# FNet mixing and a channel MLP on one core: z split untransposed, and transposed by the DMA that loads it

## The chip, the core and the metric

The kernel runs on one core of a Trainium2 chip. The metric is the device time of one execution in microseconds: the median of three runs is 1991.27 us (1990.38 to 1991.77).

## The reference

`A_x` has 2048 tokens of 1024 features; the MLP's hidden width is 3584. All is f32.

```python
mod = (silu(c) @ w_mod).reshape(1, 6, 1, 1024)
sa, ca, ga, sb, cb, gb = (mod[:, i] for i in range(6))
h = layernorm(x) * (1 + ca) + sa
a, b = h @ dft_hid_re.T, h @ dft_hid_im.T
x = x + ga * (dft_seq_re @ a - dft_seq_im @ b)
h = layernorm(x) * (1 + cb) + sb
h = layernorm(h)                                  # the MLP's own
x = x + gb * (gelu(h @ w1 + b1) @ w2 + b2)
```

## The kernel before

Every large product runs in fp16 with split operands: a f32 number is a high part (rounded to fp16) and a low part (the rest), and three matmuls (high x high, high x low, low x high) stand for one. On top of it lies one level of the Strassen-Winograd scheme: of four quadrants of each operand, sums and differences are formed on VectorE (DVE) in f32, and seven smaller products replace eight. The seven are always taken in the order 0, 1, 2, 4, 3, 6, 5.

The program has four large stages on TensorE (PE):

- gemm1 (L1112, L1162): the sequence DFT, whose result u goes to DRAM.
- gemm2 (L1394): the DFT over features, in eight blocks b of 256 tokens. A block has 14 pieces (seven products, real and imaginary) of 12 matmuls. After each block, `ln_tasks` does both layernorms of its 256 tokens on DVE and ScalarE (ACT), in the buffer `wb(b)`: two buffers of 8 KB per partition, used in turn. x is loaded into the same buffer first (`load_xw`, L1368), and added by DVE at L1253. The result, w in the code and z in the names, has tokens on the 128 partitions and 1024 features in a row, for two tiles of 128 tokens (n = 0 and 1).
- gemm3 (L1585): 28 steps g, 14 for each half of the tokens. A step multiplies 256 columns of w1 with 1024 tokens of z: seven products of 12 matmuls. w1 is the stationary operand and z the moving one, so z must have features on the partitions.
- gemm4 (L1694): after two steps of gemm3 one step of gemm4 with w2.

So z is transposed once. `turn_tile` (L1296) does it on TensorE: eight f32 transposes of 128 by 128 for a tile, with the identity `ident`, into two banks of PSUM (6 and 7 in gemm2). ACT copies the tile back (L1306, or L1864 for the last three tiles) to `zt(b, n)`. `z_tasks` then forms the quadrant sums (L411) in `zt`, and the high (L386, ACT) and low parts (L396, DVE) of the seven combinations; POOL stores each (L1328) to `zc_d[h][m]` in DRAM, h the half of the tokens and m the product. `load_zc` (L1336) loads one product's 1 MB: 128 partitions with 8 KB in a row. The first seven loads are issued while block 7 of gemm2 runs, since they go to the room of its right operands `dp`; the other seven (`reload`) while step 13 of gemm3 runs, each when that step has used the product's old contents.

The order on each engine is made when the program is built. `Task` has an engine, an estimated cost and what it depends on; streams of tasks have a due time; `pick` takes, by a model of the engines' clocks, what may start next. Loads are issued by SP in such an order, with 8 of its DMAs in flight at most (each waits for the one eight before it); stores of z by POOL. Both queues are in order. In gemm2 the function `turns` asks after every piece whether a tile of z is ready by the model, and puts its transposes there. `load_xw(b)` waits until the transposes of block b - 2 have read the buffer.

## Time and profile before

| | |
|---|---|
| median of three runs | 1991.27 us |
| profiled execution, first to last instruction | 1990.4 us |
| TensorE busy, weight loads busy | 1969.1, 896.5 us |
| DVE, ACT, POOL busy | 1417.3, 851.1, 190.5 us |
| f32 transposes | 128 (L1296) |
| gemm1, gemm2, first gemm3, first gemm4 begin | 47.4, 658.3, 961.9, 1021.2 us |
| granted TensorE clock | 0.999 |

The profiled execution has no other time than that span; the median of the runs lies 0.9 us above it. Times in the profile count from the first instruction. A line number is the one in the kernel before; in the changed kernel the same statements have numbers that are lower by 3 (up to L1279) or by 17 to 53 (after it).

### The profile page before, as it was taken

How to read it: one execution, taken by the hardware profiler on the slowest of the kernel's cores; microseconds unless marked ns; L12 is line 12 of the kernel's file. 1: busy time of each engine (PE TensorE's matmuls, PEld its weight loads, DVE VectorE, ACT ScalarE, POOL GpSimd, SP SyncE). 2: the span in 40 equal slices, each digit the busy share in tenths (PEclk: the TensorE clock that was granted, in tenths of full speed). 3: DMA queues.
4: the chain of work that ended last, by engine and by line, in shares of the span. 5: the costliest groups of instructions: out<-in, count | busy, mean ns of one | idle time of the engine just before them, and what ended most of it. 6: DMA issues, size and time to landing. Idle time of an engine off the chain costs nothing. (4 is left out here: it accounts for less than half of the span.)

```text
span 1990.4 us, 23735 instructions
## 1 busy us (share of the span) xinstructions
PE 1969.1 (99%) x9082; PEld 896.5 (45%) x9082; DVE 1417.3 (71%) x1795; ACT 851.1 (43%) x1091; POOL 190.5 (10%) x282
## 2 busy tenths in 40 slices
PE   9999999999999999999999999999999999999999
PEld 3444444444444444444444444444444444444443
DVE  2977886997984467777588999999873353553566
ACT  2853432344542245554477566466233322312311
POOL 0002212221220112221020000000000000000000
PEclk9999999999999999999999999999999999999999
DMA  9138677678779777877765454453477332432323
GB/s 380 53 97 281 236 264 275 246 298 329 249 256 364 271 261 256 282 244 277 276 218 190 171 199 168 145 175 146 169 231 216 117 97 83 127 101 69 111 74 85
DMA packets 139363, 402.42 MB, mean 202 GB/s; under 512 B 15536, under 2 KB 15536, under 8 KB 134640
## 3 DMA queue, kind: packets, MB, share of 16 engines
q1 hardware_dynamic: 112528, 309.92, 45.3%
q0 software_dynamic: 26720, 90.98, 12.8%
q8 instruction: 71, 1.16, 0.2%
q14 instruction: 44, 0.36, 0.1%
HBM read 262.95 MB, written 137.89 MB: 201 GB/s over the span
## 5 line engine op out<-in xcount | busy, mean ns | idle before, releaser
L1694 PE MATMUL ps<-arena 128*128 128x512 f16 x2352 | 511.1, 379 | 2.8 <-DVE arena L1740 1.5
L1585 PE MATMUL ps<-arena 128*128 128x512 f16 x2352 | 510.2, 379 | 2.2 <-ACT arena L1607 2.2
L1162 PE MATMUL ps<-arena 128*128 128x512 f16 x2016 | 435.5, 379 | 1.4 <-DMA arena<-s 1.4
L1694 PEld LDWEIGHTS <-arena 128*128 128x128 f16 x2352 | 229.9, 98 | 281.5 <-issue 3.8
L1585 PEld LDWEIGHTS <-arena 128*128 128x128 f16 x2352 | 230.1, 98 | 279.4 <-issue 2.5
L1740 DVE SCALAR_TENSOR_TENSOR arena<-ps,i4c,arena 128x1024 f32<-128x1024 f32 x179 | 229.3, 1281 | 144.4 <-PE ps L1694 143.1
L1162 PEld LDWEIGHTS <-arena 128*128 128x128 f16 x2016 | 197.1, 98 | 239.5 <-DMA arena<-s 1.9
L1394 PE MATMUL ps<-arena 128*128 128x512 f16 x1344 | 292.4, 379 | 1.9 <-DMA arena<-u 1.9
L386 ACT ACTIVATE arena<-arena,shc 128x512 f16<-128x512 f32 (+1 forms) x115 | 115.9, 1018 | 277.3 <-PE ps L1694 184.6
L1394 PEld LDWEIGHTS <-arena 128*128 128x128 f16 x1344 | 131.4, 98 | 158.0 <-DMA arena<-u 2.4
L1112 PE MATMUL ps<-arena 128*128 128x512 f16 x768 | 167.4, 379 | 7.2 <-ACT arena L635 2.0
L411 DVE TENSOR_TENSOR arena<-arena 128x512 f32<-128x512 f32 (+1 forms) x228 | 171.0, 753 | 4.1
L681 ACT ACTIVATE arena<-arena 128x1024 f16<-128x1024 f32 x100 | 104.1, 1050 | 150.8 <-PE ps L1162 111.4
L398 DVE SCALAR_TENSOR_TENSOR arena<-arena,shc 128x512 f16<-128x512 f32 (+1 forms) x115 | 128.7, 1122 | 38.4 <-ACT arena L386 38.3
L684 DVE SCALAR_TENSOR_TENSOR arena<-arena 128x1024 f16<-128x1024 f32 x100 | 128.6, 1303 | 18.5 <-ACT arena L681 18.5
L1611 DVE TENSOR_TENSOR arena<-arena,ps 128x512 f32<-128x512 f32 x84 | 57.5, 685 | 110.7 <-PE ps L1585 106.5
L1604 ACT ACTIVATE arena<-arena,b1s,i1c 128x512 f32<-128x512 f32 x84 | 68.3, 813 | 137.0 <-DVE arena L1611 137.0
L1112 PEld LDWEIGHTS <-arena 128*128 128x128 f16 x768 | 74.7, 98 | 99.9 <-ACT arena L635 4.0
L773 ACT ACTIVATE arena<-arena 128x1024 f16<-128x1024 f32 x56 | 57.7, 1047 | 60.9 <-DVE arena L1186 18.8
L776 DVE TENSOR_TENSOR arena<-arena 128x1024 f16<-128x1024 f32 x56 | 66.9, 1218 | 14.6 <-ACT arena L773 14.6
L386 ACT ACTIVATE arena<-arena,s1c 128x512 f16<-128x512 f32 (+1 forms) x70 | 60.8, 884 | 36.9 <-DVE arena L411 25.9
L398 DVE SCALAR_TENSOR_TENSOR arena<-arena,s1c 128x512 f16<-128x512 f32 (+1 forms) x70 | 66.3, 959 | 11.0 <-ACT arena L386 10.8
(159 smaller groups left out, 1418.8 us busy)
## 6 DMA issues: line engine op xcount, KB each, us to landing
w<-arena SPq DMA_DIRECT2D x64, 512.0 KB, 5.0
arena<-w SPq DMA_DIRECT2D x119, 256.0 KB, 2.7
u<-arena POOLq DMA_DIRECT2D x56, 512.0 KB, 5.5
arena<-u SPq DMA_DIRECT2D x112, 256.0 KB, 4.0
arena<-w SPq DMA_DIRECT2D x56, 512.0 KB, 3.4
arena<-s SPq DMA_DIRECT2D x48, 512.0 KB, 7.6
arena<-in_cre_dram SPq DMA_DIRECT2D x32, 512.0 KB, 7.3
arena<-in_cim_dram SPq DMA_DIRECT2D x32, 512.0 KB, 5.2
```

The lines of the kernel that those rows point to most:

```text
L386: act.activation(o[m][0], q(j), AF.Copy, **sc)
L398: dve.scalar_tensor_tensor(o[m][1], q(j), scale, o[m][0], op0=ALU.mult, op1=ALU.subtract)
L411: dve.tensor_tensor(q(d), q(a), q(b), op=op)
L681: h = Task("act", 1.15, lambda: act.activation(o[:, :, 0], s2, AF.Copy, scale=SC), list(deps) + free)
L684: dve.scalar_tensor_tensor(o[:, :, 1], s2, SC, o[:, :, 0], op0=ALU.mult, op1=ALU.subtract)
L1112: pe.matmul(bank_of(d_), hleft(d_, s, kp, a), cop(n)[:, s, b], start=(kp == 0 and s == 0 and a == 0 and b == 0), stop=(kp == 7 and s == 1 ...
L1162: pe.matmul(bank_of(st + ch), left, cop(n)[:, s, b], start=(start and kp == 0 and s == 0 and a == 0 and b == 0), stop=(kp == 3 and s == 1 ...
L1394: pe.matmul(bank_of(bk), up(N)[:, c_, a], dp(n)[:, c_, w], start=(start and ri == 0 and c_ == 0 and i == 0), stop=(ri == 1 and c_ == 3 and ...
L1585: pe.matmul(ps.rearrange("p (k t) -> p k t", k=4), w1c[:, m, s, a, d * P : (d + 1) * P], zc(m)[:, b, :, d, :], start=(start and d == 0 and ...
L1604: act.activation(dst, src, AF.Gelu_apprx_tanh, scale=inv, bias=b1s[:, 2 * p + j : 2 * p + j + 1])
L1694: pe.matmul(t[:, j], hidc[:, c_, m, a, k * P : (k + 1) * P], w2c[:, m, c_, w], start=(start and c_ == 0 and n == 0), stop=(c_ == 1 and n = ...
L1740: lambda: dve.scalar_tensor_tensor(dst, ps[b], inv, dst, op0=ALU.mult, op1=ALU.add), kp[b],
```

## The change

The transposes, their copies, the identity and `turns` are gone. `z_tasks` works in place on w itself, with tokens on the partitions, and the stores write that layout. For the last block the layernorm's final ACT operation writes to the place `O_K` directly, where `zt` stood before. `load_zc` issues a transposing DMA: of the 4096 columns of a product, each run of 128 becomes 128 partitions with 128 tokens. The buffer of w is then free for x only when z is split, so `load_xw(b)` waits for the seven combinations of block b - 2. `z_tasks(b)` is handed to the planner after `ln_tasks(b)`, due 40 us later, and has six places for its results.

```diff
@@ ln_tasks
-            f = lambda n=n: act.activation(w[:, n], w[:, n], AF.Identity, scale=r[:, n : n + 1], bias=nm[:, n : n + 1])
+            f = lambda n=n: act.activation(zw(b)[:, n], w[:, n], AF.Identity, scale=r[:, n : n + 1], bias=nm[:, n : n + 1])
...
-    def zt(b, n):
-        return at((O_K if b == NB - 1 else 144) + 4 * n, 1024)
-
-    def turn_tile(b, n, ps):
-
-        for d in range(ND):
-            pe.transpose(ps[:, d * P : (d + 1) * P], wb(b)[:, n, d * P : (d + 1) * P], ident[:, :])
-
-    def turn(b, n):
...
+    def zw(b):
+
+        return at(O_K, 2048).rearrange("p (r e) -> p r e", r=2) if b == NB - 1 else wb(b)
 
     def z_tasks(b):
 
-        e, o = zt(b, 0), zt(b, 1)
+        e, o = zw(b)[:, 0], zw(b)[:, 1]
...
-        places = [O_K + 8 + 2 * k for k in range(4)] if b == NB - 1 else [152, 154, 46 if b == NB - 2 else 182, 216, 218]
+        places = [O_K + 8 + 2 * k for k in range(4)] if b == NB - 1 else [144, 146, 148, 150, 152, 154]
...
-            dst = zc_d[h][m][:, :, k].rearrange("p a c t -> p a (c t)")
+            dst = zc_d[h][m][:, :, k].rearrange("p a c e -> p a (c e)")
...
-            q, outs, None, 512, lambda j: ("zt", b, j % 2), lambda m: ("z", b, m), post=post,
+            q, outs, None, 512, lambda j: ("w", b, j % 2), lambda m: ("z", b, m), post=post,
...
     def load_zc(h, m):
-        sp.dma_start(at(O_ZC[m], 4096, F16), zc_d[h][m].rearrange("p a k c t -> p (a k c t)"))
+        o = at(O_ZC[m], 4096, F16).rearrange("p (n t) -> p n t", t=P)
+        sp.dma_start_transpose(o, zc_d[h][m].rearrange("p a k c e -> p (a k c e)"))
...
-        was = [("turn", b - 2, n) for n in range(2)] if b > 1 else [("g1", opn(3, 5, 3))]
+        was = [("z", b - 2, m) for m in range(7)] if b > 1 else [("g1", opn(3, 5, 3))]
...
     for b in range(NB):
         gemm2(b, each(b))
         push("ln", "ln", ln_tasks(b), clk["pe"] + 10.0)
+        if b < NB - 2:
+            push("z", f"z{b}", z_tasks(b), clk["pe"] + 40.0)
...
-    def turn_late(b, n):
...
-                turn_late(NB - 2, 0)
                 push("z", f"z{NB - 2}", z_tasks(NB - 2), due[3, 1] + 5)
...
-                turn_late(NB - 1, 1)
-                turn_late(NB - 1, 0)
                 push("z", f"z{NB - 1}", z_tasks(NB - 1), due[4, 0] + 10)
```

How it moves the instructions is shown at three places. First SP's queue at the end of gemm2, the loads of the first half. In these names `zc_0` to `zc_6` are z's products, `w_1` is w1's step 1, `u_6_1` and the like are the last left operands of gemm2, and `in_x` is x for a layernorm (here that of block 7). Before:

```order
249 L1346 DMA arena_65<-u_6_1_140 128x1024
250 L1336 DMA arena_65<-zc_0_67 128x4096
251 L1571 DMA arena_65<-w_1_161 128x1024
252 L1368 DMA arena_65<-in_x_dram 128x2x1024
253 L1336 DMA arena_65<-zc_1_68 128x4096
254 L1571 DMA arena_65<-w_1_161 128x1024
255 L1346 DMA arena_65<-u_5_0_137 128x1024
256 L1336 DMA arena_65<-zc_2_69 128x4096
257 L1571 DMA arena_65<-w_1_161 128x1024
258 L1346 DMA arena_65<-u_5_1_138 128x1024
259 L1336 DMA arena_65<-zc_4_71 128x4096
```

And SP's queue at the same place in the changed kernel:

```order
251 L1319 DMA_TRANSPOSE arena_65<-zc_0_67 128x32x128
252 L1527 DMA arena_65<-w_1_161 128x1024
253 L1329 DMA arena_65<-u_6_1_140 128x1024
254 L1319 DMA_TRANSPOSE arena_65<-zc_1_68 128x32x128
...
256 L1329 DMA arena_65<-u_5_0_137 128x1024
257 L1319 DMA_TRANSPOSE arena_65<-zc_2_69 128x32x128
...
259 L1329 DMA arena_65<-u_5_1_138 128x1024
260 L1319 DMA_TRANSPOSE arena_65<-zc_4_71 128x32x128
...
264 L1319 DMA_TRANSPOSE arena_65<-zc_6_73 128x32x128
265 L1527 DMA arena_65<-w_1_161 128x1024
266 L1351 DMA arena_65<-in_x_dram 128x2x1024
267 L1319 DMA_TRANSPOSE arena_65<-zc_5_72 128x32x128
```

The seven loads of z are transposes now, with the same w1 loads between them; the load of x for block 7 has moved from behind the first of them to behind the sixth, and u_6_1 from ahead of the first to behind it.

Second, DVE around the last layernorm, where block 5's splits end before it (L396 low part, L411 quadrant sum, L1416 the adds of gemm2, L1267 and L1253 the first operations of block 7's layernorm, L1611 the first add of gemm3). Before:

```order
714 L1416 TENSOR_TENSOR arena_65<-arena_65,ps 128x512
715 L396 TENSOR_TENSOR arena_65<-arena_65 128x512
716 L411 TENSOR_TENSOR arena_65<-arena_65 128x512
717 L1416 TENSOR_TENSOR arena_65<-arena_65,ps 128x512
718 L411 TENSOR_TENSOR arena_65<-arena_65 128x512
719 L396 TENSOR_TENSOR arena_65<-arena_65 128x512 x3
...
727 L1253 SCALAR_TENSOR_TENSOR arena_65,lns_35_218<-arena_65 128x1024
728 L1267 TENSOR_TENSOR arena_65<-arena_65 128x1024
729 L1253 SCALAR_TENSOR_TENSOR arena_65,lns_35_218<-arena_65 128x1024
730 L1611 TENSOR_TENSOR arena_65<-arena_65,ps 128x512
```

In the changed kernel, DVE at the same place (L393 is the low part, L1399 the adds of gemm2, L1250 the add of x, L1569 the adds of gemm3):

```order
690 L393 TENSOR_TENSOR arena_65<-arena_65 128x512 x3
...
693 L1399 TENSOR_TENSOR arena_65<-arena_65,ps 128x512
...
701 L1399 TENSOR_TENSOR arena_65<-arena_65,ps 128x512
...
716 L1569 TENSOR_TENSOR arena_65<-arena_65,ps 128x512
717 L1264 TENSOR_TENSOR arena_65<-arena_65 128x1024
718 L1250 SCALAR_TENSOR_TENSOR arena_65,lns_34_213<-arena_65 128x1024
719 L1264 TENSOR_TENSOR arena_65<-arena_65 128x1024
720 L1250 SCALAR_TENSOR_TENSOR arena_65,lns_34_213<-arena_65 128x1024
721 L1212 TENSOR_SCALAR lns_34_213<-lns_34_213 128x2
722 L1569 TENSOR_TENSOR arena_65<-arena_65,ps 128x512 x2
```

The last low parts of block 5 now stand ahead of the last two adds of gemm2, and the adds of x behind the first add of gemm3 instead of ahead of it.

Third, TensorE at the end of the third gemm3 step, with the two tiles of block 7 turned before the first gemm4:

```order
8894 L1585 MATMUL ps<-arena_65 128x512
8895 L1296 MATMUL ps<-ident_181,arena_65 128x128 x16
8896 L1694 LDWEIGHTS arena_65
8897 L1694 MATMUL ps<-arena_65 128x512
```

In the changed kernel, TensorE at the same place (L1543 is gemm3, L1652 gemm4):

```order
8880 L1543 MATMUL ps<-arena_65 128x512
8881 L1652 LDWEIGHTS arena_65
8882 L1652 MATMUL ps<-arena_65 128x512
```

The 16 transposes are gone and the matmuls on both sides follow each other; the other 14 places are alike.

40 lines of the change are left out of this document (removed).

## The prediction

> **What bounds the kernel now.** I read the share of busy time first, then who made TensorE wait, then TensorE's own timeline where the change cuts into it.
>
> ```profile
> PE 1969.1 (99%) x9082; PEld 896.5 (45%) x9082; DVE 1417.3 (71%) x1795; ACT 851.1 (43%) x1091; POOL 190.5 (10%) x282
> PE ps L1585 <- ACT arena L1607: 2.2, 1, 2.2
> PE ps L1394 <- DMA arena<-u: 1.9, 1, 1.9
> PE ps L1694 <- DVE arena L1740: 1.5, 2, 1.2
> L1296 PE MATMUL ps<-ident,arena 128*128 128x128 f32 x128 | 16.4, 273 | 0.0
> L1306 ACT ACTIVATE arena<-ps 128x1024 f32<-128x1024 f32 x13 | 13.3, 1023 | 22.7 <-PE ps L1296 22.7
> ```
>
> TensorE is busy for 99% of the span, and its two longest waits (engine, line, who released it, total us) are of about 2 us each. So a microsecond taken out of TensorE's stream is a microsecond of the span, unless something else then arrives late. The 128 transposes (L1296) are in that stream. Their copies out of PSUM (L1306, and three at L1864) are on ACT, which is busy for 43%: these are not on the path.
>
> **What the transposes cost.** The mean of 273 ns is no price, because records of neighbouring matmuls overlap. The price is the distance between starts (start, length, engine, line, count):
>
> ```profile
> 771.45 1.04 PE L1296 MATMUL ps<-ident,arena 128*128 128x128 f32 x8
> 772.32 5.34 PE L1394 MATMUL ps<-arena 128*128 128x512 f16 x24
> 777.50 1.04 PE L1296 MATMUL ps<-ident,arena 128*128 128x128 f32 x8
> ...
> 932.99 23.47 PE L1394 MATMUL ps<-arena 128*128 128x512 f16 x108
> 958.38 2.76 PE L1394 MATMUL ps<-arena 128*128 128x512 f16 x12 [1.92 <-DMA arena<-u]
> 960.98 1.04 PE L1296 MATMUL ps<-ident,arena 128*128 128x128 f32 x8
> 961.86 18.29 PE L1585 MATMUL ps<-arena 128*128 128x512 f16 x84
> ...
> 1019.49 1.91 PE L1296 MATMUL ps<-ident,arena 128*128 128x128 f32 x16
> 1021.23 5.13 PE L1694 MATMUL ps<-arena 128*128 128x512 f16 x23
> ```
>
> Eight transposes take 772.32 - 771.45 = 0.87 us, sixteen take 1021.23 - 1019.49 = 1.74 us. The 24 matmuls behind the first eight take 777.50 - 772.32 = 5.18 us, or 0.216 us each, so 12 of them (one piece of gemm2, one product of gemm3) take 2.59 us. All 16 tiles: 16 x 0.87 = **13.95 us** leave TensorE.
>
> **What is added: 14 transposing loads.** No row of this trace has one, so its price T per load (1 MB, 1.05 MB in decimal) is the unknown. How late a load may be comes from where the plain ones land now:
>
> ```profile
> 935.77 0.32 SPq L1336 DMA_DIRECT2D arena<-zc  x1
> ...
> 957.77 0.32 SPq L1336 DMA_DIRECT2D arena<-zc  x1
> ```
> ```profile
> L1336 SPq DMA_DIRECT2D arena<-zc x1: 319/319/319, 957.8 to 957.8; - x1
> DMA to landing us min/median/max: 14.3/14.3/14.3
> ```
> ```profile
> 945.00:960.00 15.00, 13.08 (x62) 5.79 (x60) 9.19 (x23) 4.43 (x7) 3.75 (x6) 1.00 1.03 415
> ```
> ```profile
> L1336 SPq DMA_DIRECT2D arena<-zc x1: 320/320/320, 1425.7 to 1425.7; - x1
> DMA to landing us min/median/max: 4.8/4.8/4.8
> ```
> ```profile
> 1425.74 8.09 SPq L1336 DMA_DIRECT2D arena<-zc  x4
> ```
> ```profile
> w<-arena SPq DMA_DIRECT2D x64, 512.0 KB, 5.0
> arena<-w SPq DMA_DIRECT2D x119, 256.0 KB, 2.7
> ...
> arena<-u SPq DMA_DIRECT2D x112, 256.0 KB, 4.0
> ...
> out_dram<-arena POOLq DMA_DIRECT2D x28, 512.0 KB, 5.5
> ...
> arena<-zc SPq DMA_DIRECT2D x14, 1024.0 KB, 6.9
> ...
> arena<-in_x_dram SPq DMA_DIRECT2D x8, 1024.0 KB, 7.4
> ```
> ```profile
> 1422.96 36.42 PE L1585 MATMUL ps<-arena 128*128 128x512 f16 x168
> ```
>
> The first seven loads are issued between 935.77 and 957.77, during the last block of gemm2. The last one lands at 957.77 + 14.3 = 972.1, and its product (the seventh of the first gemm3) starts at 961.86 + 6 x 2.59 = 977.4. The DMA engines are full there (share 1.03, 415 GB/s), so a plain 1 MB costs 1.05 / 0.415 = 2.5 us of queue and 256 KB costs 0.63. A plain load into an idle queue (the first of the second half, at 1425.7) lands after 4.8 us, so about 4.8 - 2.5 = 2.3 us are latency. In the second half each load is issued when gemm3 number 13 has done that product, and is needed 84 x 0.216 = 18.1 us later, in number 14.
>
> Bounds for T: below, a plain load, 2.5 us. Above, 6.9 us, the median from issue to landing of all 14 plain loads, as if nothing overlapped. Between them lies 4.8 us, a lone load that overlaps with nothing. (The sizes below are those of the last fence: KB each, then median us to landing.) I take the middle of 2.5 and 4.8, **T = 3.65 us**: the same bytes, source rows and queue as the plain load, with something added because the output is written in runs of 128 elements and not in one run of 4096.
>
> *First half.* The first transposing load may start when the fifth piece of the last block is done (dp piece 4 lies where it lands), 5 x 2.59 = 12.95 us into the block; the seventh is needed 20 pieces in, at 51.8. In these 38.9 us the queue must do seven transposes, seven w1 loads (4.4 us), three u loads (1.9), the x load (2.5) and the latency (2.3), and share with two 512 KB stores of POOL (2.5): 7T + 13.6. It fits while T is under 3.61; beyond that TensorE waits 7T - 25.3. The seven zc stores of block 5 fall in this window today and have moved out of it, since the splits now run about a block sooner:
>
> ```profile
> 939.37 0.69 POOL L1328 DMA_DIRECT2D zc<-arena  x1 [18.07 <-ACT arena L1410]
> ...
> 956.21 2.13 POOL L1328 DMA_DIRECT2D zc<-arena  x3 [4.83 <-DVE arena L396]
> ```
>
> The u load behind today's 1.92 us wait has three transposes ahead, and x no longer: 12.95 + 3T + 1.9 + 1.9 + 2.3 = 30.0 at T = 3.65, against piece 13 at 33.7. So these **1.92 us** go as well.
>
> *Second half.* From the first issue to the seventh need are 18.1 + 6 x 2.59 = 33.7 us, for seven transposes, one 512 KB store in the same queue (1.3) and 2.3 of latency: it fits while T is under 4.30, and beyond that TensorE waits 7T - 30.1.
>
> At T = 3.65 the first half costs 0.3 us and the second nothing.
>
> **What moves.** The x load of block 7 now stands behind six transposes on SP. Behind it waits DVE, in order: the add of x (L1253), and behind that the adds of the first gemm3 (L1611), on which its seventh product waits.
>
> ```profile
> 959.13 1.23 DVE L1253 SCALAR_TENSOR_TENSOR arena<-arena 128x1024 f32<-128x1024 f32 x1
> ...
> 975.07 0.69 DVE L1611 TENSOR_TENSOR arena<-arena,ps 128x512 f32<-128x512 f32 x1 [3.29 <-PE ps L1585]
> ```
>
> It lands at 12.95 + 6T + 13.0 (six w1 loads 3.8, then 1.9 + 2.5 + 2.5 + 2.3 as above) = 47.9 us into the block; then three operations of 1.23 us and one of 0.69 end at 52.3, against 51.8 for that product: 0.5 us, in the same wait as the 0.3 and not beside it. The x loads of the other blocks wait for DVE's split in place of TensorE's turn. That split runs one block after the layernorm, and the buffer is needed two blocks after (2 x 14 x 2.59 = 72 us), so I cost this at nothing; if that cover went, DVE would wait for x as here. The splits themselves keep count and size. ACT loses 16 copies of 1.02 us, and PSUM banks 6 and 7 come free in gemm2: nothing on the path waits for either. The identity's making goes from POOL at the start, off the path.
>
> **The sum**, against this execution's span of 1990.4 us: -13.95 - 1.92 + 0.5 = -15.4. The median of the runs is 1991.27 us, 0.9 above the span; the same difference from it gives **1976 us**. At T = 2.5 nothing would be late: 1991.27 - 15.87 = 1975.4, and with the 2.2 us wait of L1585 for ACT gone too, 1973.
>
> Rows first, then a page: here 7.3 MB would have to go by at 1.05 / 3.65 = 287 GB/s in each half. The Trainium skill, "DMA: Bandwidth & Descriptors", section "Latency and other measured facts", gives 261 GB/s for a DMA transpose with a non-contiguous middle dimension; by that, as an estimate, T = 4.0, a first wait of 2.8 us and 1978 us. That page's rate is the one that speaks against the change; no run here shows a transpose yet.
>
> **The rivals.**
>
> *One at a time.* Each transpose holds the queue from issue to landing, T = 4.8: waits of 8.3 and 3.5 us, 1991.27 - 15.87 + 11.8 = 1987 us. For it: nothing in the trace shows two of them overlapping. Against: the plain loads do overlap. In the second half four are issued within 8.09 us, while one takes 4.8 to land.
>
> *The loads become the bound, slower.* It decides from T = 5.1, where both waits (14T - 55.4) eat the 15.87. At T = 6.9 the waits are 23.0 and 18.2 us, at the first products of the first and of the fifteenth gemm3: 1991.27 - 15.87 + 41.2 = 2017 us. For it: both hand-overs are tight even for plain loads (5.3 us to spare in the first), the engines are full there, and everything on SP stands behind a transpose. Against: the bytes are the same, and a price of twice the plain one is needed.
>
> *The gain does not arrive.* DVE has more to do than the time it has once TensorE is 16 us ahead, and late adds give the time back: 1988 to 1992 us. For it: DVE is busy 71% over all. Against: in the block of gemm2 quoted above it is busy for 9.19 of 15 us, and TensorE's longest wait for DVE, in the first fence, is 1.5 us in total.
>
> **How the numbers follow.** My forecast (T up to 4.3, 1974 to 1980) has 0.46, one at a time 0.11, the loads as the bound 0.36, and the gain that does not arrive 0.07. About 0.2%, 4 us, is what a measurement of this kernel can tell from no change. Faster by more: 0.46 plus 0.09 of the one-at-a-time case (T a little under 4.8) = 0.55. The same: its other 0.02 and 0.06 of the last = 0.08. Slower: 0.36 and 0.01 = 0.37. The range runs from 1973 (T = 2.5, the L1585 wait gone) to 2018 (T = 6.9); beyond it lies T above 6.9, some 0.16. Since both signs hold much of the chance: the likeliest case alone runs from 1974 to 1980.
>
> **What would show it.** Right: no L1296, 0.216 us from the last matmul of a piece to the next; the transposes' landings 3 to 4.3 us apart when they queue; TensorE's first gemm3 product straight behind gemm2, and no wait in the fifteenth gemm3. Wrong: waits of L1585 (as it is renumbered) for a transpose of zc in the first and the fifteenth gemm3, of 7T - 25.3 and 7T - 30.1; DVE waiting for x at the add of the last layernorm; or SP busy for microseconds in issuing one transpose, with the u and w1 loads late behind it, which would sink the forecast however fast the DMA engines are.

## The result: slower, by 17.5 us

| | before | after |
|---|---|---|
| median of the runs | 1991.26 us (1990.38 to 1991.77) | 2008.74 us (2008.09 to 2009.17) |
| ratio, 95% interval | | 1.0085 (1.0071 to 1.0100) |
| profiled span | 1990.4 us | 2006.3 us |
| first gemm3 / first gemm4 / 14th gemm3 / 7th gemm4 begin | 961.86 / 1021.23 / 1422.96 / 1459.22 us | 960.59 / 1032.61 / 1432.51 / 1474.80 us |
| granted TensorE clock | 0.999 | 0.992 |

The forecast was 1976 us, the range 1973 to 2018. The time lies in the range, and on the side of the rival in which the loads become the bound. The profiled run took 2008.09 us, 1.8 us more than its span. The runs of the kernel before that list both exceed their spans by about as much, so its profiled execution was, as an estimate, 0.9 us slower than its median: the spans differ by 15.9 us, the medians by 17.5.

The 128 transposes are gone from TensorE: its stream has 8954 instructions where it had 9082. The page of the changed kernel (busy time and share of the span first, then the slices 1 to 40 of the granted clock) and its packet count:

```profile
PE 1964.1 (98%) x8954; PEld 883.5 (44%) x8954; DVE 1418.4 (71%) x1795; ACT 835.0 (42%) x1075; POOL 189.7 (9%) x280
...
PEclk9999999999999999999889999999999999999999
...
DMA packets 195136, 402.39 MB, mean 201 GB/s; under 512 B 73104, under 2 KB 73104, under 8 KB 192208
```

Busy time fell by only 5 us, though 14 us of work left: the two 8s in the clock, from 953 to 1053 us, say that matmuls ran slower there. Packets under 512 bytes are 73104; the page before has 15536. The difference of 57568 is 14 x 4096 and a remainder of 14 x 16. So a transposing load moves its 1 MB in 4096 packets, which makes 256 bytes each.

The waits of TensorE in the changed kernel (engine, line, who released it, total us, times, longest):

```profile
PE ps L1543 <- ACT arena L1565: 8.9, 1, 8.9
PE ps L1377 <- DMA arena<-u: 8.3, 2, 4.4
PE ps L1543 <- DVE arena L1569: 4.8, 1, 4.8
PE ps L1543 <- DMA arena<-zc: 3.9, 2, 3.0
```

Four causes, 26 us together, where these stages of the kernel before had two of about 2 us. TensorE's timeline shows where they lie, and what follows each (start, length, matmuls, wait ahead):

```profile
947.17 4.19 PE L1377 MATMUL ps<-arena 128*128 128x512 f16 x12 [3.93 <-DMA arena<-u]
955.74 5.01 PE L1377 MATMUL ps<-arena 128*128 128x512 f16 x12 [4.39 <-DMA arena<-u]
960.59 15.70 PE L1543 MATMUL ps<-arena 128*128 128x512 f16 x72
981.12 27.57 PE L1543 MATMUL ps<-arena 128*128 128x512 f16 x120 [4.83 <-DVE arena L1569]
1017.63 15.14 PE L1543 MATMUL ps<-arena 128*128 128x512 f16 x60 [8.94 <-ACT arena L1565]
1032.61 36.42 PE L1652 MATMUL ps<-arena 128*128 128x512 f16 x168
...
1432.51 28.65 PE L1543 MATMUL ps<-arena 128*128 128x512 f16 x132
1464.19 7.10 PE L1543 MATMUL ps<-arena 128*128 128x512 f16 x24 [3.03 <-DMA arena<-zc]
1472.20 2.76 PE L1543 MATMUL ps<-arena 128*128 128x512 f16 x12 [0.91 <-DMA arena<-zc]
```

In the kernel before, the third step of gemm3 waited for ACT too, but for 2.21 us:

```profile
1006.54 13.11 PE L1585 MATMUL ps<-arena 128*128 128x512 f16 x60 [2.21 <-ACT arena L1607]
```

Twelve matmuls took 2.76 us in the kernel before, also behind its 1.92 us wait. Behind waits of 3.9 and 4.4 us they take 4.19 and 5.01. The reason is the clock, in the windows of the changed kernel (from:to, length, busy time of PE, PEld, DVE, ACT, POOL, granted clock, DMA share, GB/s):

```profile
943.00:960.00 17.00, 8.68 (x25) 2.94 (x24) 3.85 (x10) 1.95 (x4) 1.10 (x2) 0.71 1.11 293
```

and the same window of the kernel before:

```profile
943.00:960.00 17.00, 15.08 (x71) 6.69 (x70) 10.86 (x26) 5.88 (x9) 4.60 (x7) 1.00 1.03 414
```

The clock was 0.71 there and 1.00 before. The last two columns of each row show the other half of the story: in both the DMA engines count as full, but now at 293 GB/s, not 414.

The queue of SP in the changed kernel, where it issues the first half's loads (start, length of the issue, line, operation), then the second half's:

```profile
925.13 5.68 SPq L1319 DMA_TRANSPOSE arena<-zc  x1
...
932.10 8.05 SPq L1319 DMA_TRANSPOSE arena<-zc  x1
940.20 0.58 SPq L1527 DMA_DIRECT2D arena<-w  x1
940.82 0.43 SPq L1329 DMA_DIRECT2D arena<-u  x1
941.41 7.20 SPq L1319 DMA_TRANSPOSE arena<-zc  x1
948.72 0.52 SPq L1527 DMA_DIRECT2D arena<-w  x1
949.28 0.92 SPq L1329 DMA_DIRECT2D arena<-u  x1
950.37 7.06 SPq L1319 DMA_TRANSPOSE arena<-zc  x1
...
970.57 0.39 SPq L1351 DMA_DIRECT2D arena<-in_x_dram  x1
...
1435.29 19.09 SPq L1319 DMA_TRANSPOSE arena<-zc  x4
...
1455.11 14.92 SPq L1319 DMA_TRANSPOSE arena<-zc  x3
```

A plain load of z was issued in 0.32 us. A transposing one holds SP for 5.2 to 8.1 us in the first hand-over and for 34.01 / 7 = 4.86 us on average in the second, and everything behind it in the queue stands still. The u loads that TensorE waits for could not be issued before 940.82 and 949.28, and x not before 970.57. DVE in the changed kernel stood for it:

```profile
976.63 1.23 DVE L1250 SCALAR_TENSOR_TENSOR arena<-arena 128x1024 f32<-128x1024 f32 x1 [8.84 <-DMA arena<-in_x_dram]
```

Behind that add stand, in order, the adds of gemm3 (L1569) that TensorE waits 4.83 us for at 981.12.

So the span can be added up, by rows of the two timelines:

| term | forecast | measured | from |
|---|---|---|---|
| 16 turned tiles off TensorE | -13.95 | -13.95 | no L1296; the price is that of the kernel before |
| u | -1.92 | +6.40 | 3.93 + 4.39 - 1.92 |
| x, through DVE's adds | +0.5 | +4.83 | 981.12 |
| ACT's copy in the third step of gemm3 | 0 | +6.73 | 8.94 - 2.21 |
| z, second half | 0 | +3.94 | 3.03 + 0.91 |
| matmuls at a lower clock behind these waits | 0 | +8.98 | (4.19 - 2.76) + (5.01 - 2.76) + (27.57 - 26.06) + (15.14 - 13.11) + (7.10 - 5.34) |
| the rest | 0 | -1.0 | gemm2 begins 1.1 us earlier, at 657.19 |
| sum | -15.4 | +15.9 | 2006.3 - 1990.4 |

(The 26.06 us for 120 matmuls at full clock come from the first experiment's timeline, 13.11 for 60 and 5.34 for 24 from that of the kernel before.)

### The profile page after: what moved, and what is told of

It is laid out like the page before. It is cut to its first block, busy times and chain, and to the rows that moved or that the text cites. A ratio compares the mean times of both kernels' runs of the same rounds, so it can differ in the third digit from the quotient of the medians.

```text
span 2006.3 us, 23428 instructions
## 1 busy us (share of the span) xinstructions
PE 1964.1 (98%) x8954; PEld 883.5 (44%) x8954; DVE 1418.4 (71%) x1795; ACT 835.0 (42%) x1075; POOL 189.7 (9%) x280
## 2 busy tenths in 40 slices
DMA packets 195136, 402.39 MB, mean 201 GB/s; under 512 B 73104, under 2 KB 73104, under 8 KB 192208
## 3 DMA queue, kind: packets, MB, share of 16 engines
q1 hardware_dynamic: 168304, 309.92, 47.0%
## 4 chain that ended last, share of the span: by engine, by line
PE 84%; DVE 9%; DMA 3%; issue 2%; ACT 1%; SPq 0%; POOL 0%; DVEq 0%; POOLq 0%; ACTq 0%
PE ps L1543 23%; PE ps L1652 23%; PE ps L1159 18%; PE ps L1377 13%; PE ps L1109 5%; DVE arena L681 1%; PE ps L471 1%; DVE arena L630 1%; DVE arena L631 1%; DVE arena L395 1%; DMA arena<-zc 1%; DVE arena L1698 1%; DVE arena L633 1%; DMA arena<-in_wm_dram 1%; PE ps L477 1%
## 5 line engine op out<-in xcount | busy, mean ns | idle before, releaser
L1543 PE MATMUL ps<-arena 128*128 128x512 f16 x2352 | 515.9, 382 | 17.7 <-ACT arena L1565 8.9
L1652 PE MATMUL ps<-arena 128*128 128x512 f16 x2352 | 510.8, 379 | 1.3 <-DVE sums L908 0.5
L1543 PEld LDWEIGHTS <-arena 128*128 128x128 f16 x2352 | 231.0, 98 | 300.5 <-issue 16.5
L1652 PEld LDWEIGHTS <-arena 128*128 128x128 f16 x2352 | 229.9, 98 | 279.9 <-issue 1.7
L383 ACT ACTIVATE arena<-arena,shc 128x512 f16<-128x512 f32 (+1 forms) x115 | 115.9, 1018 | 276.5 <-PE ps L1652 184.6
L1569 DVE TENSOR_TENSOR arena<-arena,ps 128x512 f32<-128x512 f32 x84 | 57.5, 686 | 110.9 <-PE ps L1543 105.9
L773 DVE TENSOR_TENSOR arena<-arena 128x1024 f16<-128x1024 f32 x56 | 66.9, 1219 | 14.7 <-ACT arena L770 14.7
L383 ACT ACTIVATE arena<-arena,s1c 128x512 f16<-128x512 f32 (+1 forms) x70 | 60.7, 884 | 37.0 <-DVE arena L408 24.2
L1565 ACT ACTIVATE arena<-ps 128x512 f32<-128x512 f32 x84 | 49.7, 592 | 59.2 <-PE ps L1543 58.0
```

The lines of the kernel that those rows point to most:

```text
L383: act.activation(o[m][0], q(j), AF.Copy, **sc)
L1543: pe.matmul(ps.rearrange("p (k t) -> p k t", k=4), w1c[:, m, s, a, d * P : (d + 1) * P], zc(m)[:, b, :, d, :], start=(start and d == 0 and ...
L1652: pe.matmul(t[:, j], hidc[:, c_, m, a, k * P : (k + 1) * P], w2c[:, m, c_, w], start=(start and c_ == 0 and n == 0), stop=(c_ == 1 and n = ...
```

## The experiments

Each time below is a median with its lowest and highest; each ratio is to the kernel before on the same chip, with its 95% interval.

### Both halves loaded plainly

```diff
     def load_zc(h, m):
-        o = at(O_ZC[m], 4096, F16).rearrange("p (n t) -> p n t", t=P)
-        sp.dma_start_transpose(o, zc_d[h][m].rearrange("p a k c e -> p (a k c e)"))
+        sp.dma_start(at(O_ZC[m], 4096, F16), zc_d[h][m].rearrange("p a k c e -> p (a k c e)"))
```

> Leaves out the transposing: both halves of z are loaded by the plain DMA, untransposed, so gemm3 multiplies with z as it lies; all else is the changed kernel. Theory A (all of the loss comes from the 14 transposing loads): the 13.95 us of transposes and the 1.9 us wait for u are gone and nothing is late, 1975 us, within 2. Rival B (the loss comes from the new order of the splits, the layernorm and the x loads): the waits of gemm3 for DVE and ACT stay, 1985 us or more.

1982.61 us (1982.21 to 1983.56), ratio 0.9952 (0.9935 to 0.9968). So the transposing loads cost 2008.74 - 1982.61 = 26 us, and the rest of the change, which should have given 1975.4, gives 7 us less than that. Its timeline:

```profile
947.16 15.70 PE L1542 MATMUL ps<-arena 128*128 128x512 f16 x72
963.69 26.06 PE L1542 MATMUL ps<-arena 128*128 128x512 f16 x120 [0.83 <-DVE arena L1568]
998.69 15.62 PE L1542 MATMUL ps<-arena 128*128 128x512 f16 x60 [8.93 <-ACT arena L1564]
```

The first gemm3 starts 961.86 - 947.16 = 14.7 us earlier than before: the gain is there. (2.5 us of it lie ahead of gemm2, which begins at 655.86 here and at 658.33 before; why is left open. Gemm2 itself is 12.2 us shorter.) The u waits and the x wait are gone or small (0.83). But the wait for ACT's copy is the same 8.93 us without any transpose in the way. From the first gemm3 to the first gemm4 the kernel before took 59.4 us, 2.6 of them transposes; this one takes 1014.14 - 947.16 = 67.0. Its ACT shows what stands in front of the copy (L1564):

```profile
985.29 1.14 ACT L383 ACTIVATE arena<-arena,shc 128x1024 f16<-128x1024 f32 x1
986.33 1.14 ACT L383 ACTIVATE arena<-arena 128x512 f16<-128x512 f32 x2
987.57 2.37 ACT L1276 ACTIVATE arena<-arena,lns 128x1024 f32<-128x1024 f32 x2
991.76 1.67 ACT L383 ACTIVATE arena<-arena 128x512 f16<-128x512 f32 x3 [1.83 <-DVE arena L408]
993.34 1.00 ACT L892 ACTIVATE ps<-arena 128x1024 f32<-128x1024 f32 x1
...
998.06 0.58 ACT L1564 ACTIVATE arena<-ps 128x512 f32<-128x512 f32 x1
```

That is the end of the last layernorm (L1276), block 6's splits (L383) and the squares of a norm of w1 (L892). From the last gelu of the step before (at 984.61) to the copy it takes 13.4 us, 2.5 of them waits for DVE. In the kernel before the same stretch, from 999.23 to 1005.91, took 6.7 us, because the layernorm's last operations stood further ahead and the squares behind the copies.

### The second half alone transposed

```diff
-        o = at(O_ZC[m], 4096, F16).rearrange("p (n t) -> p n t", t=P)
-        sp.dma_start_transpose(o, zc_d[h][m].rearrange("p a k c e -> p (a k c e)"))
+        src = zc_d[h][m].rearrange("p a k c e -> p (a k c e)")
+        if h == 0:
+            sp.dma_start(at(O_ZC[m], 4096, F16), src)
+        else:
+            sp.dma_start_transpose(at(O_ZC[m], 4096, F16).rearrange("p (n t) -> p n t", t=P), src)
```

> Leaves out the transposing in the first half alone (plain loads there); the second half is loaded by transposes as in the changed kernel. By the stage times of the changed kernel the second half costs 1474.80 - 1459.22 - (1432.51 - 1422.96) = 6.0 us against the kernel before. Theory A: 1975.4 + 6.0 = 1981.5 us, and no wait in gemm2 or the first gemm3 for u, x or zc. If the two halves did not add up (each slows the other), the result would be off that by more than 2 us.

1992.18 us (1989.71 to 1996.91), ratio 1.0005 (0.9995 to 1.0016). Against the kernel with both halves plain, the second half's transposes cost 9.6 us, the first half's therefore the other 16.5. TensorE waits 4.22, 0.68 and 1.84 us for z in the fifteenth gemm3, and the 12 matmuls behind the first of these take 4.22 us, not 2.76. The time is 10.7 us over the expected 1981.5: 7 of them are what the plain kernel also lacked, with the same 8.94 us wait for ACT, and the second half cost 9.6 us here and not the 6.0 of the changed kernel's stages. So the split of the 26 us between the halves is good to some 4 us only.

### The loads that are late put ahead

The last u loads are issued ahead of the first transpose, x behind the fourth, and w1's loads behind the seventh.

```diff
-                if 4 <= n < 11:
+                if n == 5:
+                    emitted(*(("up", NP * b + j) for j in range(NP)))
+                    load_zc(0, ORDER[0])
+                if n == 8:
+                    need("z5")
+                    emitted(("xw", b))
+                if 5 <= n < 11:
                     load_zc(0, ORDER[n - 4])
-                    m = ORDER[n - 4]
-                    sp.dma_start(w1c[:, m, 1], w1_d[1][:, m])
-                    done["w1", 1, m] = clk["pe"]
+                if n == 10:
+                    for m in ORDER:
+                        sp.dma_start(w1c[:, m, 1], w1_d[1][:, m])
+                        done["w1", 1, m] = clk["pe"]
```

> The changed kernel with another order on SP in the last block of gemm2: the last u loads ahead of the first transpose, the x load of block 7 behind the fourth transpose and not the sixth, the seven w1 loads of step 1 behind the last; the first transpose one piece (2.59 us) later. Output complete. Theory A1 (SP is held for some 5 us by issuing one transpose, and the loss is what stands behind it on SP): the waits for u (8.3 us) and for x (4.8, and 8.9 that follows) go, the seventh product waits some 0 to 3 us, the second half costs 6.0: 1981 to 1985 us. Rival A2 (the DMA engines are what is slow, and the order changes little, because what moves ahead takes the same engines' time from the transposes): 1990 us or more, with waits for zc in the first gemm3.

2006.94 us (2003.17 to 2009.71), ratio 1.0068 (1.0044 to 1.0093). The waits for u are gone, and behind x (DVE itself still waits 11.30 us for it) TensorE waits only 0.77 us for DVE's add, but now it waits for z itself:

```profile
959.82 6.77 PE L1550 MATMUL ps<-arena 128*128 128x512 f16 x24 [6.24 <-DMA arena<-zc]
971.80 5.00 PE L1550 MATMUL ps<-arena 128*128 128x512 f16 x12 [5.21 <-DMA arena<-zc]
977.68 2.76 PE L1550 MATMUL ps<-arena 128*128 128x512 f16 x12 [0.87 <-DMA arena<-zc]
```

6.24 + 5.21 + 0.87 = 12.3 us. In the changed kernel it was 8.3 for u and 4.83 - 0.83 = 4.0 for x, also 12.3. In both orders the queue has too much work, and the order decides who waits. Back to back the first four transposes held SP for 8.2 us each, the last three for 5.7:

```profile
928.18 32.99 SPq L1319 DMA_TRANSPOSE arena<-zc  x4
961.28 0.53 SPq L1351 DMA_DIRECT2D arena<-in_x_dram  x1
961.99 17.14 SPq L1319 DMA_TRANSPOSE arena<-zc  x3
```

### The price of one transpose

Six transposes that nobody reads, in quiet late steps of the kernel before: 4096 columns, 2048, 1024, and three of 2048 in a row.

```diff
+            if v in (8, 9, 10, 11):
+                for kb, cols in {8: [(136, 4096)], 9: [(136, 2048)], 10: [(136, 1024)], 11: [(136, 2048), (140, 2048), (216, 2048)]}[v]:
+                    o = at(kb, cols, F16).rearrange("p (n t) -> p n t", t=P)
+                    sp.dma_start_transpose(o, zc_d[0][0].rearrange("p a k c t -> p (a k c t)")[:, 0:cols])
```

> The kernel before, with six more transposing loads into unused room in late steps of the second half (gemm4 steps 8 to 11), where the DMA engines are less than half busy: one of 4096 columns, one of 2048, one of 1024, and three of 2048 in a row. Nothing reads what they load. Theory A1 (issuing is the work of SP, by column): SP is held for 4.8, 2.4 and 1.2 us, in proportion, though the engines are free, and each lands some 2.4 us after its issue has ended. Rival A2 (SP only waits for full engines): the issue of the small ones is well under 1 us, as for a plain DMA (0.32 us), and the landing takes the time.

```profile
1604.12 5.21 SPq L1935 DMA_TRANSPOSE arena<-zc  x1
...
1676.64 3.15 SPq L1935 DMA_TRANSPOSE arena<-zc  x1
...
1749.16 1.24 SPq L1935 DMA_TRANSPOSE arena<-zc  x1
```

The hold of SP grows with the columns: 5.21, 3.15 and 1.24 us, or 1.2 to 1.6 us per 1024. Each lands 2.1 to 2.4 us after its issue ends, as the 2.3 us of latency of a plain load. During the first, the windows of this kernel show the DMA engines at a share of 1.04 with 194 GB/s:

```profile
1604.50:1609.50 5.00, 5.00 (x25) 2.28 (x24) 1.84 (x2) 0.04 (x1) 0.00 (x0) 1.00 1.04 194
```

### Is it SP or the DMA engines?

In a first attempt the kernel before got 3 MB of stores on POOL beside such transposes.

> The kernel before with extra traffic in four quiet late steps of gemm4, whose results nobody reads: in one step 3 MB of plain stores from POOL alone; in another one 1 MB transpose on SP alone; in two steps both together. Theory A (a transpose is bound by how fast SP issues its pieces): it holds SP for 5.2 us beside the stores as without them. Theory B (it is bound by the DMA engines, which its 256-byte packets fill): beside the stores it holds SP for 8 us or more, as in the first hand-over, and the stores land later than without it.

It was inconclusive on the question: POOL's queue was ahead, and its stores were over by about 1550 us, before the first transpose at 1678.92. The three transposes, then without company, held SP for 5.35, 5.24 and 4.96 us. In a second attempt SP issues both, so that they fall together:

```diff
+            if v in (8, 9, 10, 11):
+                for k in range({8: 3, 9: 3, 10: 0, 11: 3}[v]):
+                    sp.dma_start(spare_d[k][:, :], at(O_ZC[k], 4096, F16))
+                if v > 8:
+                    o = at(136, 4096, F16).rearrange("p (n t) -> p n t", t=P)
+                    sp.dma_start_transpose(o, zc_d[0][0].rearrange("p a k c t -> p (a k c t)"))
```

> The kernel before with extra traffic in four quiet late steps of gemm4, all of it issued by SP so that it falls together, and read by nobody: three 1 MB stores alone in the first; three stores and right behind them one 1 MB transpose in the second and the fourth; one transpose alone in the third. Theory A (a transpose is bound by how fast SP issues its pieces): it holds SP for 5.0 to 5.4 us behind the stores as without them. Theory B (it is bound by the DMA engines): behind the stores, which alone need some 7.5 us at 415 GB/s, it holds SP for 8 us or more and lands later than 10 us from its issue.

```profile
1676.81 2.09 SPq L1935 DMA_DIRECT2D spare<-arena  x3
1678.95 11.19 SPq L1938 DMA_TRANSPOSE arena<-zc  x1
...
1749.33 5.13 SPq L1938 DMA_TRANSPOSE arena<-zc  x1
...
1823.97 11.17 SPq L1938 DMA_TRANSPOSE arena<-zc  x1
```

Alone 5.13 us, behind 3 MB of stores 11.19 and 11.17. So the hold is not SP's own work alone: SP waits for what stands ahead. The stores stood in SP's own queue, and no run has them on another queue at the same moment, so this does not tell that queue from the engines behind it. What speaks for the engines is their busy share beside one transposing load alone: 1.04 above, and 0.92 to 0.98 for the four lone issues of these two kernels, at 186 to 194 GB/s. The time of the packets on SP's queue points the same way, though coarsely: for the same 309.92 MB it is 917 us of all engines with both halves plain (46.3% of the span), 933 with the second transposed (46.9%), 943 with both (47.0%), but 902 in the kernel before (45.3%). By that reading a transposing megabyte costs about 5.1 us of all the DMA engines, twice the plain 2.5 us, on top of whatever else they have to do; it fits that the same load held SP for 4.9 us on average in the second half and for 5.2 to 8.1 us in the first.

### Transposing elsewhere

If the price is the engines' time, it may be paid where TensorE waits for nothing. Five kernels turn z in 56 small transposes (256 KB each), store it turned, and load it plainly in the hand-overs. In the first, the blocks 0 to 4 are turned from SBUF to SBUF right behind their split, the others in steps 4 to 10 of gemm3:

```diff
         def post(m, o_):
...
+            def f():
+                sp.dma_start_transpose(tt.rearrange("p (n t) -> p n t", t=P), o_[2].rearrange("p a x -> p (a x)"))
+                gp.dma_start(dst, tt.rearrange("p (a x) -> p a x", a=2))
+
+            store("z", (b, i), f, ("z", b, m), f"z{b}")
```

> The same untransposed splits, but the DMA transposes are taken out of the hand-overs: 56 small ones (128 x 1024, 256 KB each) instead of 14 large ones. For blocks 0 to 4 each follows its split in gemm2 and goes from SBUF to SBUF, for blocks 5 to 7 they go from DRAM during steps 4 to 10 of gemm3; the result is stored to DRAM turned, and loaded plainly in the two hand-overs as in the kernel before. Theory A (a transpose costs only where it delays a load that TensorE waits for): the time is that of the plain, unturned loads, 1980 to 1986 us; each issue holds SP for 1.2 to 2 us; ACT's 8.9 us wait stays. Theory B (56 holds of SP and the extra pass of 14 MB through the engines cost wherever they are): u or w loads come late in gemm2 and gemm3, and the time is 1990 or more.

> The staged kernel with the last u loads and the x load ahead in SP's queue, and with block 6's splits and the last layernorm issued inside the third step of gemm3 behind its fifth product. If the three costs (transposing loads at the hand-overs, the late x, ACT's order) are separate and add up: 1983 less 6 to 8 for ACT's order and up to 1 for x, 1974 to 1977 us, with TensorE's longest wait under 3 us around the first gemm4. If the last layernorm's chain bounds the first three steps of gemm3 whatever the order: 1981 to 1984.

They took 2057.50 us (2052.21 to 2058.92), ratio 1.0325 (1.0307 to 1.0343), and 2057.36 us (2056.64 to 2058.22), ratio 1.0328 (1.0310 to 1.0345). TensorE waits in gemm2 for ACT (22.6 us in the first), whose splits find no free place (the chain that ended last runs there through transposes and their stores), and in gemm4 for DVE (24.4). I took that for the design's fault, not the transposes', and spread them out: the splits store to DRAM as in the changed kernel, and each small transpose follows three blocks later, one in every other piece (blocks 0 to 3), or in every other product of steps 4 to 10 (the rest); POOL stores the turned piece one slot later.

```diff
+    def turn(b, m, place):
+        store_turned()
+        tt = at(place, 1024, F16)
+        sp.dma_start_transpose(tt.rearrange("p (n t) -> p n t", t=P), zs_d[b, m][:, :])
+        dst = zc_d[b // 4][m][:, :, b % 4].rearrange("p a c t -> p a (c t)")
+        behind.append(lambda: gp.dma_start(dst, tt.rearrange("p (a x) -> p a x", a=2)))
```

> The staged kernel spread out so that SP, ACT and DVE have nothing to wait for: the splits store untransposed to DRAM exactly as in the changed kernel; the 56 small transposes (DRAM to SBUF, 256 KB) follow three blocks later, one every other piece of gemm2 (blocks 0 to 3, three places in turn), or one every other product of steps 4 to 10 of gemm3 (blocks 4 to 7, two places), and POOL stores each turned piece one slot later. Both hand-overs load plainly. Theory A (the earlier staged kernel lost its 66 us to full places: ACT's splits and SP stood behind a transpose and its store): no wait in gemm2 and in steps 4 to 10, and the time is that of the plain, unturned loads, 1981 to 1987 us, with ACT's 8.9 us wait still there. Theory B (small transposes cost SP and the DMA engines too much wherever they are): u, w1 or w2 come late, 1995 us or more.

2029.97 us (2021.85 to 2039.59), ratio 1.0193 (1.0149 to 1.0236): the waits for ACT in gemm2 were still 32.5 us. With the turned pieces stored by SP (`sp` for `gp` in the last line):

> The spread kernel with one difference: the turned pieces are stored by SP, one slot behind their transpose, and not by POOL, so that the stores of the splits on POOL no longer stand behind a transpose's landing. Theory A (the spread kernel's 21 and 9 us waits for ACT in gemm2 are POOL's queue: the split's place comes free only when POOL's store behind a turned store is done): those waits go, and the time comes down from 2030 to 1983 to 1990 us. Theory B (14 MB of transposes in 256-byte packets cost wherever they are): the waits move to u, w1 or w2, and the time stays over 1995.

2056.18 us (2050.74 to 2062.93), ratio 1.0328 (1.0297 to 1.0358); and with u, x and two other operations moved besides:

> The kernel with the turned pieces stored by SP and with the same three mends (u, x, and the two deferred things). If the small transposes are hidden and the mends work as in the plain kernel: 1976 to 1982 us, which beats the kernel before by about 0.5%. If transposes cost wherever they are: 1990 or more.

2048.07 us (2042.94 to 2053.33), ratio 1.0286 (1.0254 to 1.0317). One more kernel, the spread one with u and x ahead and the same two operations later, took 2029.78 us (2026.89 to 2036.42) where 1974 to 1980 were expected; its output is not the reference's, so that time says only that it gains nothing. With SP's stores TensorE waits for u (19.4 us in the first of the two) and still for ACT (10.8). Whoever stands in a queue behind the DMA engines waits, and the windows suggest the reason. First the kernel before, in the middle of gemm2, then the one that stores by SP:

```profile
820.00:860.00 40.00, 40.00 (x195) 19.15 (x193) 32.21 (x58) 21.74 (x35) 8.78 (x14) 1.00 0.73 260
```
```profile
820.00:860.00 40.00, 30.55 (x125) 12.71 (x124) 18.89 (x36) 15.20 (x27) 4.75 (x9) 0.87 1.05 288
```

The DMA engines are at 0.73 there before any transpose, and at 0.78 over all of gemm2. A block of gemm2 takes 14 x 2.59 = 36.3 us; seven small transposes of about 1.3 us and seven more stores of 0.63 add, as an estimate, 13.4 us to it, or 0.37. That makes 1.10, and there is no room for it. (No kernel tells this from SP's holds, which all loads of u stand behind.) TensorE's 99% had hidden a second resource that is three quarters used. No place for these transposes was found at which the kernel gains. The quiet late steps are no such place: z's second half is needed from the fifteenth gemm3 on, ahead of them.

### ACT's wait

The other 7 us. First, what must be issued between the second and the third step of gemm3 (the end of block 6's splits and of the last layernorm, then w2's first loads) was put inside the third step, behind its fifth product:

```diff
+    def second(m):
+        if m == 3:
+            need(f"z{NB - 2}", "ln", "st_w2", "st_x2")
...
```

> The changed kernel with one thing moved: what stands between the second and the third step of gemm3 (the end of block 6's splits and of the last layernorm, which must be issued before w2's first loads) is issued inside the third step, behind its fifth product, so that ACT's three copies for that step stand ahead of it. Theory A (ACT's order makes the 8.9 us wait): the wait of the third step's third product for ACT falls from 8.9 us to under 3, the matmuls behind it run at full clock, and the time falls by 6 to 9 us from 2008.7, to about 2001; the waits for u and zc stay. Theory B (the last layernorm is late in itself, and what follows it is needed anyway): the wait moves to the adds of that step or to the first products of gemm4, and the time stays at 2006 or more.

2012.61 us (2009.39 to 2013.29), ratio 1.0101 (1.0086 to 1.0116). The wait for ACT's copy fell from 8.9 to 1.3 us, and in its place came 3.12 us for an add of DVE and 4.22 us for w2, whose loads my edit had moved too; the first gemm4 began only 1.6 us earlier. Next, with plain loads again, two things that are not urgent were deferred (the squares L892, and the last layernorm's two keeps on DVE, which set the result aside for the last sum), and u and x put ahead. The edit also moves two of w2's first loads into the third step and w1's loads of step 1 behind z's:

> The changed kernel with both halves loaded plainly and so not transposed (as in the first of the experiments), with the last u loads and the x load of block 7 ahead on SP, and with the norm of w1's step 3 and the last layernorm's two keeps issued later, behind ACT's first copy of the third step of gemm3. Theory A (these 2.9 us of squares on ACT and 2.4 us of keeps on DVE make most of the 8.9 us wait, and the late x the 0.8 us one): the wait falls to 3 or 4 us and the time from 1982.6 to 1976 to 1978 us. Theory B (the last layernorm is late whatever stands beside it): the wait stays at 7 us or more, or comes back at the adds of that step or the first products of gemm4, and the time stays within 2 us of 1982.6.

1990.60 us (1986.61 to 1992.37), ratio 0.9994 (0.9985 to 1.0004), 8 us more than with plain loads alone. ACT's wait fell from 8.9 to 7.0 us, and 5.5 us for ACT appeared in the first gemm4, with 2.1 us of slow matmuls behind them, and 2.3 us for DVE in the third. Then the reason for the late layernorm: x of block 7 can only be loaded when block 5's splits have freed its buffer. With a buffer of its own (block 5's splits are then also due 25 us later, and those of blocks 5 and 6 have other places):

```diff
-        return at(O_W + 8 * (b % 2), 2048).rearrange("p (r e) -> p r e", r=2)
+        return at(144 if b == 7 else O_W + 8 * (b % 2), 2048).rearrange("p (r e) -> p r e", r=2)
...
-        was = [("z", b - 2, m) for m in range(7)] if b > 1 else [("g1", opn(3, 5, 3))]
+        was = [("z", min(b - 2, 4), m) for m in range(7)] if b > 1 else [("g1", opn(3, 5, 3))]
...
```

> The changed kernel with both halves loaded plainly and so not transposed, and with a buffer of its own for x of block 7 (8 KB a partition that the split's places had; blocks 5 and 6 get five other places): its load no longer waits for block 5's splits, it is issued early in block 7, and these splits are due 25 us later, behind the layernorm of block 6. Theory A (the freed buffer is what makes the last layernorm late, and that the 8.9 us wait): DVE's wait for x is gone, the last layernorm's first add starts within 4 us of gemm2's end as in the kernel before, ACT's wait falls under 4 us, and the time falls from 1982.6 to 1975 to 1978 us. Theory B (only what stands in front of ACT's copy counts, and that is nearly the same here): x comes early but the 8.9 us wait stays within 1.5 us, and the time within 2 us of 1982.6.

> The kernel with a buffer of its own for x of block 7, loaded plainly and not transposed, and besides with the norm of w1's step 3 and the last layernorm's keeps issued behind ACT's first copy of the third step of gemm3. If both hold (late x, and what stands in front of the copy): ACT's wait under 3 us and 1974 to 1977 us. If this work only moves: the wait falls and others of the same sum appear in the first gemm4, 1981 us or more.

1980.90 us (1980.41 to 1981.12), ratio 0.9945 (0.9928 to 0.9961), and with the two deferred things 1980.62 us (1978.97 to 1982.00), ratio 0.9943 (0.9928 to 0.9958). DVE no longer waits for x, the add of x starts at 951.20, and the wait is 7.4 and 4.9 us:

```profile
996.99 14.56 PE L1542 MATMUL ps<-arena 128*128 128x512 f16 x60 [7.43 <-ACT arena L1564]
```
```profile
995.02 15.91 PE L1542 MATMUL ps<-arena 128*128 128x512 f16 x60 [4.91 <-ACT arena L1564]
```

So the late x is worth some 2 of the 7 us: 1.7 by the medians, which come from two chips and whose intervals overlap as ratios, and 3.5 by the profiles, from the start of gemm2 to the first gemm4. Taking work from in front of the copy shortens this wait by another 2.5 us, but the 60 matmuls behind it take 15.91 us and no longer 14.56, and the gemm3 behind the first gemm4 begins at 1047.64 in both. What is left open is whether another order of ACT and DVE in this stretch would win the other 5; three that I tried did not. None of the kernels that do the whole computation beat the kernel before.

## Why the prediction was wrong, by its own steps

*What bounds the kernel, and what leaves.* Right. With plain loads gemm2 is 12.2 us shorter; 13 of the 16 tiles (11.3 us) and the 1.92 us wait of u lie in it, less a new 1.1 us wait for ACT.

*The price T.* **This is the step that failed: "the same bytes, source rows and queue as the plain load", T = 3.65, the middle of 2.5 and 4.8.** Issued alone, beside w2's loads, one held SP for 4.96 to 5.35 us in five cases. I took the bytes to be the price. What differs is the packets: 4096 of 256 bytes per load, and the DMA engines count as full at 194 GB/s, less than half of the plain 415. That the packets are the reason is argued from this; no run has transposes with other packets. The point from which the loads decide was in the text, T = 5.1, with the objection that "a price of twice the plain one is needed". It is twice: 5.13 / 2.5 = 2.05. With the waits and the slow matmuls behind them, the transposing loads cost 26 us.

The Trainium skill, "DMA: Bandwidth & Descriptors", section "Latency and other measured facts", gives 261 GB/s for a transpose with a non-contiguous middle dimension, T = 4.0 as an estimate; that was nearer than my middle and still short, for 1.05 MB in 5.13 us are 205 GB/s. If source rows of 8 KB in one piece, as here, are its contiguous case, the same row of the Trainium skill gives about 350 to 400 GB/s, and the trace is further from that.

*The two formulas.* The second held. 7T - 30.1 with the mean hold of the second half, 4.86 us, gives 3.9 us; measured 3.94. In the kernel with the second half alone transposed it gives 6.5 at its mean of 5.23; measured 6.74. The first fell short: 7T - 25.3 gives 8.7 us at 4.86 and 10.6 at 5.13, and measured were 12.3, as z's waits where z was put last and as u's and x's waits in the changed kernel. One of its premises failed: that block 5's seven stores of zc "have moved out" of this window. POOL issues them right behind the first transposing load (925.13):

```profile
925.44 1.40 POOL L1310 DMA_DIRECT2D zc<-arena  x2 [11.92 <-DVE arena L393]
...
936.28 1.39 POOL L1310 DMA_DIRECT2D zc<-arena  x2 [1.29 <-issue]
```

The splits run 14 to 22 us sooner, not a block of 36. At the 0.63 us that the prediction has for 256 KB the seven stores add 4.4 us, which makes 7T - 20.9: 13.1 us at 4.86, 15.0 at 5.13. That is worked out afterwards, and no run takes these stores out. The place was wrong too. I had only z wait, and counted the u wait as gone, by its landing in a queue in which issues cost nothing.

*u and x.* The list of what would prove the forecast wrong had "SP busy for microseconds in issuing one transpose, with the u and w1 loads late behind it"; u and x were. The formula for u had 3T in it and was right about the queue; at T = 3.65 it left 3.7 us of room, and at the 5.7, 8.1 and 7.2 us of the first three holds it leaves none. x cost 4.83 us of TensorE, not 0.5.

*"I cost this at nothing": the splits' new order.* Wrong by 6.7 us. I argued from the x loads of the other blocks and from DVE's busy share. x of block 7 has to wait for block 5's splits, which makes the last layernorm later (some 2 us by the experiment), and in the changed order ACT, 43% busy before and 42% now, has a stretch of 13.4 us in front of one copy. A mean share says nothing about a queue at a hand-over. I had this as a rival, "the gain does not arrive", named DVE for it, and gave it 0.07. It was right in kind, and it came beside the others and not instead of them: I had set rivals against each other that add up.

*What no step had: the clock.* Of the waits in the sum, the five from 3.03 us on are followed by slow matmuls, 9.0 us in all, on 25 us of waits. The timelines of all kernels here, from gemm2 on, say more (at full clock a row of n matmuls is n x 0.216 + 0.17 us long). Behind waits of 2.21, 2.30 and 2.45 us nothing was lost; behind ten of the fifteen from 2.48 to 3.23 us 1.4 to 1.9 us were, behind the other five none; behind every one from 3.31 to 21 us 1.3 to 3.2 us, and not more for the longer ones. The Trainium skill, "TensorE: Matmul & The Clock Gate", Part 1, says that the clock falls to half after an idle window of about 3.4 us and comes back after as long a busy one. By that, as an estimate, each such wait costs another 1.7 us; the mean of the five is 1.8. The traces agree with it for the waits of 3.3 us and more; that ten shorter ones cost as much, it does not say. A forecast of waits near 3 us or over should carry this term.

*The rivals.* The loads as the bound was the one that came true, at T = 5.1 and not at 6.9: by its formulas 1991.27 - 15.87 + 16.0 = 1991 us. Most of the other 17 us are ACT's wait (6.7) and the clock (9.0), which no rival had. *One at a time*, with 1987 us, had the price nearly right (4.8, where the holds of the second half have 4.86) and SP's queue held, though a load lands 2.1 us or more after its hold has ended; it lacked block 5's stores, ACT's wait and the clock as well.

## What to carry to other kernels

When work moves from an engine to the DMA engines, read their busy share in the windows where it will land, and look at the packets too, not only at the bytes: here a transposing load took twice the time of a plain one, and a share of 0.73 to 1.03 left no room for it in gemm2. A DMA that is issued slowly is a wait for everything behind it in its queue; list those loads and who needs them first. Price a new wait of TensorE of some 3 us or more with about 2 us of slow matmuls behind it, and let rivals add up where they have different places.

## What the runs showed that was not expected

- A transposing DMA holds the issuing queue for microseconds (1.24 us for 256 KB, 5.0 to 5.4 us for 1 MB, 11.2 us behind 3 MB of stores); a plain one is handed over in 0.32 us.
- Its source rows are 8 KB long, and still its packets are 256 bytes, 4096 per MB.
- Matmuls behind every wait of 3.31 us or more ran slower, for 1.3 to 3.2 us whatever the length (12 in 4.19 and 5.01 us, where 2.76 is full speed; a granted clock of 0.71 in that window); behind 2.45 us or less they did not, and between the two both were seen.
- The waits moved and kept their sum in the two orders that were run: 12.3 us in the first hand-over, for u and x in one, for z in the other.
